# A written plan for the attention steps of the late tiles, on one core

## The chip, the cores and the metric

The kernel runs on one core of a Trainium2 chip. The metric is the time of one execution on the device in microseconds (us), as the median of several runs. Profiles show one execution; PE is TensorE, DVE VectorE, ACT ScalarE, POOL GpSimd, SP SyncE.

## The reference

Pooled attention feeds two feed-forward layers, all in float32:

```python
# q, k, v: 4 batches, 8 heads, 576 positions, 64 per head; pool 8, so 72 pooled keys
k_p = k.reshape(B, H, 72, 8, D).mean(axis=3)
v_p = v.reshape(B, H, 72, 8, D).mean(axis=3)
scores = scale * q @ k_p.T
attn = exp(scores - max(scores)); attn = attn / (sum(attn) + 1e-9)
x = (attn @ v_p), heads side by side            # 2304 tokens x 512
x = (sigmoid(x @ w_gate) * (x @ w_val)) @ w_out # 512 -> 1536 -> 512
h = x @ w_in                                    # 512 -> 2048
out = (h * tanh(softplus(h))) @ w_out2          # 2048 -> 512
```

## The kernel before

The 2304 tokens are 18 attention tiles of 128 tokens, and for the first feed-forward layer five blocks `j` of 512, 384, 384, 512 and 512 tokens (L68). Every large matrix product is made of three products of high and low parts. Block `j` runs 12 units `f` (`NF`), one for each 128 columns of the hidden layer. A unit (L886 to L921) is three parts: the gate product `pg` (12 matmuls, L583 to L587) and its sigmoid on ACT (L893); the value product `pv` (12 matmuls), the gating product on DVE (L899), the high part `gh` on ACT (L902) and the low part `gl` on DVE (L906); and the out product of the unit before (`emit_out`, 12 matmuls, L103 to L105). `pg` and `pv` take two PSUM buffers in turn (`ps_mm`, `bufs=2`).

After each part stand `step(j, f, k)` (L797) and `slot(3f+k)` (L851): 36 parts in a block. `step` first calls `flush` (L553), which runs what is in `later` and moves `soon` to `later`; so a thing put into `soon` in a part's slot is run two parts later, one put into `later` one part later. In blocks 2 and 3 `step` also converts the second layer's weights, one in four parts: `l` loads a raw tile on SP (L209), `c` scales it on ACT (L223), `a` joins its bits on DVE (L232, L237), `b` stores it on SP.

`slot` runs attention for the tiles of block j+1 while block j is computed. In block 0 it follows a plan written by hand (`START`). In blocks 1 to 3 it takes a list of tasks (`att_tasks`, L523, and `batch_tasks`, L360, for the keys and values of a new batch) and spreads it evenly over the 36 parts. A tile's tasks are, in order: scores on PE and row extremes on DVE (L407, L418); exponentials on ACT (L430); normalisation on DVE (L441 to L444); `att_planes`, which clears a tile on DVE (L503) and splits the 32-bit numbers into 16-bit halves on ACT (L506); two empty tasks, in which `att_turn` (L508) issues a transposing DMA on SP; `att_join` on ACT (L521), which joins the halves again; an empty task; and `att_values_out` (L481), the product with the values on PE for one or two tiles and their split into high and low parts. A batch's keys are loaded (L270), summed in groups of 8 on DVE (L276) and scaled (L280); its values are loaded (L346) and summed on DVE (L354) or POOL (L356 to L358). Key loads, value loads and queries have two buffers each.

The raw weights, the planes (`pl`), the transposed planes (`plt`) and the blocks' results (`xs`) share three buffers of one tag, `raw`. All loads and stores of these stages, the first layer's out weights (`wo`, L591) among them, are issued on SP in the order of the program.

In block 1 the old list put the steps into these parts: scores of tile 7 and keys 0, 1 loaded in 1, exponentials in 2, normalisation, keys 0, 1 pooled and keys 2, 3 loaded in 4, split in 5, keys 2, 3 pooled in 6, join in 9, values out in 12. In block 2, for tile 11: scores 8, exponentials 9, normalisation 10, split 11, transpose 13, join 14, values out of tiles 10 and 11 in 16; for tile 13: 26, 27, 28, 29, 31, 32, 34.

## Time and profile before

| what | value |
|---|---|
| median of 3 runs | 898.4 us (895.49 to 900.6) |
| profiled execution | 894.53 us, its span 892.6 us |
| granted clock of PE | 1.00 |
| busy in the span | PE 877.4, DVE 527.7, ACT 457.2, POOL 82.4 us |
| blocks 1, 2, 3 of the first layer | 138 to 222, 222 to 306, 306 to 411 us |

A timeline row gives the start, the duration, the engine, the line, the operation with its output and inputs, the shape and how many instructions are merged in it. What stands in brackets at the end is the idle time of that engine just before it, and whom it waited for. Rows of PE overlap, because matmuls are pipelined: what one costs is the distance from start to start.

### The profile page before, as it was taken

The page shows a single profiled execution, that of the slowest core. Times are in us where ns is not written, and L with a number is a line of the kernel's source. Part 1 is how long each engine was busy: PE and PEld are TensorE (multiplying, and loading weights), DVE is VectorE, ACT ScalarE, POOL GpSimd, SP SyncE. Part 2 cuts the span into 40 slices and gives each one's busy share as a digit, 9 for nine tenths or more (in the row PEclk, how much of TensorE's full clock was granted, in tenths as well). Part 3 has the DMA queues.
Part 4 walks back from the last instruction along what each step waited for, and adds up shares of the span by engine and source line. Part 5 has one row for each costly group of instructions (what it writes and reads, how often), then busy time and mean ns, then how long its engine had stood idle before and what let it go on. Part 6 is the DMA issues. An engine that isn't in the chain of part 4 may idle for free.

```text
span 892.6 us, 12631 instructions
## 1 busy us (share of the span) xinstructions
PE 877.4 (98%) x4692; PEld 781.6 (88%) x4692; DVE 527.7 (59%) x1001; ACT 457.2 (51%) x1035; POOL 82.4 (9%) x90
## 2 busy tenths in 40 slices
PE   8999999999989999999999999999999999999998
PEld 8877889899979988888888899998899998999986
DVE  6889864432644433332668477776677767677632
ACT  7756664355565656454445344455444445444431
POOL 3566430200020000000000000000000000000000
PEclk9999999999999999999999999999999999999999
DMA  7788753744686656345675231212021203110001
GB/s 271 231 301 265 223 189 131 192 134 132 171 264 191 203 167 215 120 119 189 212 242 172 70 122 47 81 48 70 26 83 48 83 24 95 60 48 24 1 35 36
DMA packets 65241, 119.08 MB, mean 133 GB/s; under 512 B 28700, under 2 KB 33564, under 8 KB 65180
## 3 DMA queue, kind: packets, MB, share of 16 engines
q1 hardware_dynamic: 63884, 116.02, 41.4%
q10 hardware_dynamic: 1296, 2.26, 0.7%
q8 instruction: 37, 0.61, 0.3%
q14 instruction: 24, 0.20, 0.1%
HBM read 92.42 MB, written 20.07 MB: 126 GB/s over the span
## 4 chain that ended last, share of the span: by engine, by line
PE 86%; ACT 5%; DMA 4%; DVE 3%; issue 1%; POOL 0%; SPq 0%; ACTq 0%; DVEq 0%
PE acc L966 22%; PE p L105 7%; PE p L103 7%; PE p L104 7%; PE acc L103 5%; PE acc L104 5%; PE acc L105 5%; PE pv L583 4%; PE pg L583 4%; PE pg L584 4%; PE pv L584 4%; PE pv L587 4%; PE pg L587 4%; ACT e L430 2%; PE pv L463 2%; PE sc L407 1%
## 5 line engine op out<-in xcount | busy, mean ns | idle before, releaser
L966 PE MATMUL acc<-w,g 128*128 128x512 f32 x864 | 201.1, 390 | 0.0
L966 PEld LDWEIGHTS acc<-w,g 128*128 128x128 f32 x864 | 161.9, 188 | 32.6
L899 DVE TENSOR_TENSOR sg<-sg,pv 128x512 f32<-128x512 f32 (+1 forms) x58 | 36.5, 629 | 124.4 <-PE pv L587 104.9
L103 PE MATMUL acc<-gh,wo 128*128 128x512 f32 (+1 forms) x240 | 90.0, 375 | 0.0
L104 PE MATMUL acc<-gl,wo 128*128 128x512 f32 (+1 forms) x240 | 88.6, 369 | 0.6 <-DVE gl L744 0.6
L583 PE MATMUL pv<-xh,wv 128*128 128x512 f32 (+1 forms) x232 | 85.8, 370 | 2.7 <-DVE sg L899 2.7
L583 PE MATMUL pg<-xh,wg 128*128 128x512 f32 (+1 forms) x232 | 86.3, 372 | 2.1 <-ACT sg L893 2.1
L105 PE MATMUL acc<-gh,wo 128*128 128x512 f32 (+1 forms) x240 | 88.3, 368 | 0.0
L584 PE MATMUL pg<-xl,wg 128*128 128x512 f32 (+1 forms) x232 | 85.2, 367 | 0.0
L584 PE MATMUL pv<-xl,wv 128*128 128x512 f32 (+1 forms) x232 | 85.1, 367 | 0.0
L902 ACT CAST gh<-sg 128x512 fp32r<-128x512 f32 (+1 forms) x60 | 34.8, 580 | 89.0 <-DVE sg L899 89.0
L103 PE MATMUL p<-top,w2s 128*128 128x384 f32 x216 | 72.5, 336 | 0.0
L105 PE MATMUL p<-top,w2s 128*128 128x384 f32 x216 | 72.4, 335 | 0.0
L104 PE MATMUL p<-top,w2s 128*128 128x384 f32 x216 | 72.3, 335 | 0.0
L893 ACT ACTIVATE sg<-pg 128x512 f32<-128x512 f32 (+1 forms) x58 | 31.9, 550 | 65.4 <-PE pg L587 65.2
L237 DVE SCALAR_TENSOR_TENSOR cv<-raw,cv 128x512 uint32<-128x512 uint32 x68 | 55.9, 822 | 2.3
L587 PE MATMUL pv<-xh,wv 128*128 128x512 f32 (+1 forms) x232 | 56.9, 367 | 0.0
L587 PE MATMUL pg<-xh,wg 128*128 128x512 f32 (+1 forms) x232 | 56.9, 367 | 0.0
L223 ACT ACTIVATE cv<-raw 128x512 f32<-128x512 f32 x66 | 44.8, 679 | 22.9 <-DMA raw<-wo 6.5
L906 DVE TENSOR_TENSOR gl<-sg,gh 128x384 fp32r<-128x384 f32 (+1 forms) x48 | 31.5, 656 | 40.0 <-ACT gh L902 40.0
L583 PEld LDWEIGHTS pv<-xh,wv 128*128 128x128 f32 x232 | 43.6, 188 | 9.4 <-DVE sg L899 3.7
L103 PEld LDWEIGHTS acc<-gh,wo 128*128 128x128 f32 x240 | 45.1, 188 | 6.7 <-issue 1.1
(153 smaller groups left out, 1693.8 us busy)
## 6 DMA issues: line engine op xcount, KB each, us to landing
wo<-wod SPq DMA_DIRECT2D x48, 512.0 KB, 4.9
ws<-w2d SPq DMA_DIRECT2D x24, 512.0 KB, 3.7
raw<-w2i SPq DMA_DIRECT2D x16, 512.0 KB, 3.9
raw<-w2o SPq DMA_DIRECT2D x16, 512.0 KB, 3.5
raw<-wv SPq DMA_DIRECT2D x12, 512.0 KB, 5.6
raw<-wo SPq DMA_DIRECT2D x12, 512.0 KB, 4.4
wod<-wo SPq DMA_DIRECT2D x12, 512.0 KB, 2.6
raw<-wg SPq DMA_DIRECT2D x11, 512.0 KB, 4.2
```

The costliest lines, as they stand in the source:

```text
L103: nc.tensor.matmul(ps, wt[:, 0, cols], xh, start=start, stop=False)
L104: nc.tensor.matmul(ps, wt[:, 0, cols], xl, start=False, stop=False)
L105: nc.tensor.matmul(ps, wt[:, 1, cols], xh, start=False, stop=stop)
L223: eng.activation(out=f32(c), in_=hi, func=AF.Prelu, scale=BIAS, alpha=-(2.0**32))
L237: nc.vector.scalar_tensor_tensor(out=c, in0=lo, scalar=29, in1=c, op0=ALU.logical_shift_right, op1=ALU.bitwise_or)
L583: nc.tensor.matmul(ps[:, c0:c1], w, xh[:, k, c0:c1], start=(k == 0), stop=False)
L584: nc.tensor.matmul(ps[:, c0:c1], w, xl[:, k, c0:c1], start=False, stop=False)
L587: nc.tensor.matmul(ps[:, c0:c1], w, xh[:, k, c0:c1], start=False, stop=(k == KD - 1))
L893: nc.scalar.activation(out=sg, in_=pg[:, :n], func=AF.Sigmoid)
L899: nc.vector.tensor_mul(out=sg, in0=sg, in1=pv[:, :n])
L902: nc.scalar.copy(out=gh, in_=sg)
L966: nc.tensor.matmul(acc[t][0], g[:, a, c], w[:, b, :], start=(f == 0 and first), stop=(f == NF2 - 1 and last),)
```

## The change

The lists of tasks of blocks 1 to 3 are replaced by three written plans of 36 parts, `LATE`. Parts are divided by `|`; a word is a step and its tile (or batch) with a number. `L` loads a key tile, `K` pools it; `U` loads a value tile, `V` sums it (`:p` on POOL, `:v` on DVE); `m`, `M`, `X`, `N` are scores, extremes, exponentials, normalisation; `Q` loads a query tile; `z` clears the planes, now on POOL; `s` splits into them on ACT and puts the transpose into `later`, not `soon`; `j7.0` and `j7.1` are the two halves of a join; `P` is the product with the values. Scores and exponentials of tiles 10 and 14 move to the end of the block before. The first raw load of the second layer's weights moves from part 3 to part 0 of block 2, and each further one from the part of the scaling of the one before (`cl`) to the part in which that one's bits are joined (`al`), so that a load stands three parts ahead of its scaling, not four.

```diff
+LATE = (
+    """
+L2.0 L2.1 m7.0 M7.0 m7.1 M7.1 | X7.0 X7.1 Q9 z7 | N7:v | s7 | K2.0:v | K2.1:v L2.2 L2.3 | U2.0 U2.1
+| j7.0 | j7.1 m8.0 M8.0 m8.1 M8.1 | X8.0 X8.1 Q10 z8 | N8:v K2.2:v | s8 K2.3:v | P7 V2.0:p V2.1:v
+U2.2 U2.3 |  |  | j8.0 V2.2:p V2.3:v U2.4 U2.5 | j8.1 | m9.0 M9.0 m9.1 M9.1 | X9.0 X9.1 Q11 z9 |
+N9:v V2.4:p V2.5:v U2.6 U2.7 | s9 |  | V2.6:p V2.7:v |  |  | j9.0 | j9.1 |  | P8.9 |  |  |  |  |  |
+m10.0 M10.0 m10.1 M10.1 | X10.0 X10.1 Q12
+""",
+    """
+L3.0 L3.1 | N10:v | z10 | s10 | K3.0:v | K3.1:v L3.2 L3.3 | U3.0 U3.1 | j10.0 | j10.1 m11.0 M11.0
+m11.1 M11.1 | X11.0 X11.1 Q13 z11 | N11:v K3.2:v | s11 K3.3:v | V3.0:p V3.1:v U3.2 U3.3 |  | j11.0 |
+j11.1 V3.2:p V3.3:v U3.4 U3.5 | m12.0 M12.0 m12.1 M12.1 | X12.0 X12.1 Q14 z12 | N12:v | s12 | P10.11
+V3.4:p V3.5:v U3.6 U3.7 |  | j12.0 V3.6:p V3.7:v | j12.1 | m13.0 M13.0 m13.1 M13.1 | X13.0 X13.1 Q15
+z13 | N13:v | s13 |  |  | j13.0 | j13.1 |  | P12.13 | m14.0 M14.0 m14.1 M14.1 | X14.0 X14.1 Q16
+""",
+    """
+ | N14:v | z14 | s14 |  |  |  | j14.0 | j14.1 m15.0 M15.0 m15.1 M15.1 | X15.0 X15.1 Q17 z15 | N15:v
+| s15 |  |  | j15.0 | j15.1 | m16.0 M16.0 m16.1 M16.1 | X16.0 X16.1 z16 | N16:v | s16 | P14.15 |  |
+j16.0 | j16.1 | m17.0 M17.0 m17.1 M17.1 | X17.0 X17.1 z17 | N17:v | s17 |  |  | j17.0 | j17.1 |  |
+P16.17 |  |
+""",
+)
...
+            def att_clear(T):
+
+                planes[T] = words("planes")
+                nc.gpsimd.memset(planes[T].bitcast(U32)[:, :, :, SP // 2 :], 0)
+
+            def att_split(T):
+
                 e = e_t[T].bitcast(U16).rearrange("p h (k w) -> p h w k", w=2)
-                h = slice(4 * g, 4 * g + 4)
-                nc.scalar.copy(out=pl_t[T][:, h, :, :SP], in_=e[:, h])
+                for h in (slice(0, 4), slice(4, 8)):
+                    nc.scalar.copy(out=planes[T][:, h, :, :SP], in_=e[:, h])
+                later.append(lambda: att_turn(T))
...
                     i = 3 * f + k + 3 * NF * (j - NBLK + 3)
-                    if i == 3:
-                        w2_step("l")
-                    elif i % 4 == 3 and pos2["c"] < NF2:
-                        w2_step("cl")
+                    if i % 4 == 3 and pos2["c"] < NF2:
+                        w2_step("c")
                     elif i % 4 == 0:
-                        w2_step("a")
+                        w2_step("al" if pos2["l"] <= NF2 else "a")
                     elif i % 4 == 1:
                         w2_step("b")
...
+                if not last:
+                    rows = plan[1:] if j == 0 else [part.split() for part in LATE[j - 1].split("|")]
...
+                    for word in rows[k]:
+                        run(word, j + 1)
```

## Rows read from the trace of the kernel before

**Rows 1.** Busy time by stage: stretch, length, then busy us of PE, PEld, DVE, ACT, POOL.
```profile
138.00:222.00 84.00, 82.03 (x505) 80.39 (x504) 31.85 (x63) 40.84 (x101) 6.31 (x12) 1.00 0.51 144
222.00:306.00 84.00, 79.97 (x487) 77.05 (x485) 38.16 (x80) 51.26 (x128) 7.25 (x12) 1.00 0.69 196
306.00:411.00 105.00, 105.00 (x546) 88.20 (x544) 38.30 (x72) 59.01 (x138) 0.00 (x0) 1.00 0.55 169
```

**Rows 2.** Timeline of PE (start, us, group; idle before in brackets): undisturbed steps.
```profile
152.28 0.85 PE L587 MATMUL pg<-xh,wg 128*128 128x384 f32 x4
152.97 0.33 PE L583 MATMUL pv<-xh,wv 128*128 128x384 f32 x1
...
216.83 1.97 PE L463 MATMUL pv<-pt,vb 72*64 72x128 f32 x32
218.73 0.44 PE L103 MATMUL acc<-gh,wo 128*128 128x384 f32 x1
```

**Rows 3.** Timeline of PE: the five places where it waits in blocks 1 and 2.
```profile
158.52 0.86 PE L587 MATMUL pg<-xh,wg 128*128 128x384 f32 x4
161.35 0.45 PE L583 MATMUL pv<-xh,wv 128*128 128x384 f32 x1 [1.98 <-DVE sg L899]
...
249.34 0.86 PE L587 MATMUL pg<-xh,wg 128*128 128x384 f32 x4
250.92 0.44 PE L583 MATMUL pv<-xh,wv 128*128 128x384 f32 x1 [0.72 <-DVE sg L899]
...
255.04 0.34 PE L105 MATMUL acc<-gh,wo 128*128 128x384 f32 x1
256.57 0.45 PE L583 MATMUL pg<-xh,wg 128*128 128x384 f32 x1 [1.20 <-ACT sg L893]
...
260.96 1.09 PE L463 MATMUL pv<-pt,vb 72*64 72x128 f32 x16
...
264.93 0.44 PE L103 MATMUL acc<-gh,wo 128*128 128x384 f32 x1
...
300.52 0.34 PE L105 MATMUL acc<-gh,wo 128*128 128x384 f32 x1
301.78 0.44 PE L583 MATMUL pg<-xh,wg 128*128 128x384 f32 x1 [0.93 <-ACT sg L893]
```

**Rows 4.** Timeline of DVE at 159 us.
```profile
159.53 0.75 DVE L276 TENSOR_REDUCE kp<-kr 128x72 f32<-128x576 f32 x1 [1.69 <-DMA kr<-kt]
```

**Rows 5.** Timeline of ACT, 244 to 300 us.
```profile
244.43 2.66 ACT L521 COPY pt<-plt 72x512 uint16<-72x512 uint16 x4 [2.21 <-DMA plt<-pl]
246.96 0.48 ACT L893 ACTIVATE sg<-pg 128x384 f32<-128x384 f32 x1
247.45 1.28 ACT L430 ACT_TABLE_LOAD   x1
...
253.47 1.25 ACT L506 COPY pl<-e 128x576 uint16<-128x576 uint16 x2 [1.22 <-DVE e L444]
...
256.03 0.49 ACT L893 ACTIVATE sg<-pg 128x384 f32<-128x384 f32 x1
...
261.88 2.63 ACT L521 COPY pt<-plt 72x512 uint16<-72x512 uint16 x4 [4.23 <-DMA plt<-pl]
...
290.93 0.66 ACT L223 ACTIVATE cv<-raw 128x512 f32<-128x512 f32 x1
...
298.68 1.25 ACT L506 COPY pl<-e 128x576 uint16<-128x576 uint16 x2 [2.86 <-DVE e L444]
```

**Rows 6.** Tile plt, output of the transposing DMA: last line of its answer.
```profile
DMA to landing us min/median/max: 4.3/4.6/7.8
```

**Rows 7.** Timeline of SP: a raw load's issue.
```profile
261.88 0.33 SPq L211 DMA_DIRECT2D raw<-w2i  x1
```

**Rows 8.** Tile raw, the loaded weights: last line of its answer.
```profile
DMA to landing us min/median/max: 3.1/3.9/7.9
```

**Rows 9.** Lines view of POOL: its largest memset (busy, mean ns, idle before).
```profile
L621 POOL MEMSET kb<- 128x576 f32 x2 | 1.1, 577 | 0.0
```

More of the change, by code (lines that the diff above doesn't have):

```diff
@@ L691, in run @@
                     first = a and a[0] < 4
+                    if op in "zsjP":
+                        if op == "z":
+                            att_clear(*a)
+                        elif op == "s":
+                            att_split(*a)
+                        elif op == "j":
+                            att_join(*a)
+                        else:
+                            att_values_out(a, j)
+                        return
                     if op == "L":
@@ L814, in tile_pooled_attention_moe_mish @@
                 last = j == NBLK - 1
-                tasks = []
-                if j == 0:
-                    ready.add(1)
-                elif not last:
-                    o2, n2 = blocks[j + 1]
-                    at = 0
-                    for b in range(o2 // S, (o2 + n2 - 1) // S + 1):
-                        if b not in ready:
-                            ready.add(b)
-                            more = batch_tasks(b)
-                            at = 0 if b * S // 128 == o2 // 128 else len(more)
-                            tasks += more
-                    rows = att_tasks(j + 1)
-                    if at:
-                        both = [y + x for x, y in zip_longest(tasks, rows, fillvalue=[])]
-                        tasks = both
-                    else:
-                        tasks += rows
+                if not last:
+                    rows = plan[1:] if j == 0 else [part.split() for part in LATE[j - 1].split("|")]
                 else:
```

101 lines of the change are left out of this document (23 added, 78 removed).

## The prediction

> **What bounds the kernel now.** I read three views in this order: the busy times by stage, the timeline of PE wherever it shows idle time, and the timelines of ACT, DVE and SP just ahead of those places. The stages first: in unit block 1 (138 to 222 us) PE is busy 82.03 of 84 us, in block 2 (222 to 306 us) 79.97 of 84 us, in block 3 (306 to 411 us) all 105 us [rows 1]. So PE is the bound, the change leaves its instructions as they are, and what can be won is PE's waiting: 1.97 + 4.03 = 6.0 us of visible idle time, all of it in blocks 1 and 2. The second view gives the true size, since a pipelined matmul's row runs on into the gap. Undisturbed, four 384-column matmuls take 0.69 us from start to start, 0.173 us each, and the value product of two tiles takes 218.73 - 216.83 = 1.90 us [rows 2]. Against that cadence the five places lose [rows 3]:
>
> - at 159 us: 161.35 - 158.52 - 0.69 = 2.14 us;
> - at 250 us: 250.92 - 249.34 - 0.69 = 0.89 us;
> - at 255 us: 256.57 - 255.04 - 0.17 = 1.36 us;
> - at 261 us: 264.93 - 260.96 - 1.90 = 2.07 us (the value product);
> - at 301 us: 301.78 - 300.52 - 0.17 = 1.09 us.
>
> That is 7.55 us. I add nothing for the restart of PE after a wait.
>
> **Why PE waits there.** The third view names a cause for each. At 159 us DVE stands 1.69 us on the load of the third or fourth key tile, with the gate product (L899) behind it [rows 4]; the old plan pooled two keys, issued the next two loads and pooled those two parts later. At 250 us ACT stood 2.21 us on the transposing DMA, and the whole join of 2.66 us with the sigmoid behind it came late [rows 5]. At 255 us that delay is still there: sigmoid, exponentials and split stand in one run on ACT, and the run that began at 246.96 delivers the next unit's sigmoid at 256.03 + 0.49 = 256.52, 9.56 us later [rows 5]. At 261 us the join waits 4.23 us for its transpose and the value product two parts behind it has to wait too [rows 5]. At 301 us a weight scaling (0.66 us at 290.93) goes ahead of the exponentials, and the split waits 2.86 us for DVE, which worked on a weight's bits ahead of the normalisation [rows 5].
>
> **The change, part by part.** *Keys.* The new plan loads two keys in part 0, pools them in parts 4 and 5, loads the next two in part 5 and pools them in parts 10 and 11. A part is 12 matmuls of 0.173 us, 2.08 us [rows 2], so even the nearest pair (part 5 to part 10) has 10.4 us. The 2.14 us go.
>
> *Exponentials, normalisation, split.* A unit is three parts, 6.24 us. Gate and value products share two `mm` buffers, so a unit's sigmoid must be done when the next unit's gate product starts, two parts (4.16 us) after its own has ended. For a run on ACT that begins with one unit's sigmoid and ends with the next one's the deadline is 6.24 + 4.16 = 10.4 us after the first gate product's end. The tightest chain of the new plan (X in the first part of a unit, N in the second, s in the third: tiles 8, 9 and 11) is the run that took 9.56 us [rows 5]. So it has 0.84 us to spare if its first sigmoid is on time. The old run at 246.96 began late, behind the join; in the new plan the join of the tile before is over a part earlier. The scaling now falls behind the exponentials, where ACT waits for the normalisation anyway, and DVE's bit work falls behind the normalisation. 1.36 and 1.09 us go, on a margin of 0.84 us. In block 3 a unit is 512 columns wide and the margin grows by a third of 10.4 us.
>
> *Join and value product.* The transpose goes out one part after the split, not two, and the first half of the join follows three to five parts after the split. Transposes landed after 4.3 to 7.8 us, median 4.6 [rows 6]. For tiles 11, 12 and 13 the DMA's issue and the half join stand at least two parts, 4.2 us, apart plus what ACT is behind; the median transpose then arrives about when ACT gets there. The value product comes three to six parts after the first half join, where before it came two parts after the whole, so the 2.07 us go even if a join waits 4 us; the join cut in halves (1.33 us each, of 2.66 [rows 5]) puts a sigmoid between, so 0.89 us go as well.
>
> *Memset on POOL.* Eleven clears leave DVE for POOL, one part or so ahead of their split. POOL is busy 6.31 and 7.25 us of 84 [rows 1] and its largest memset took 0.58 us [rows 9], so they are free as long as POOL is not standing on something else: in front of a clear stand at most some value sums waiting for loads issued three parts earlier. If that cover is gone, the split and the next sigmoid wait: 0 to 0.6 us each, 0 taken.
>
> *Raw weights.* The load now goes out three parts ahead of its scaling, 6.24 us in block 2, against 3.1 to 7.9 us of landing, median 3.9 [rows 8]. It stands on SP directly behind the transpose of the same part, and it needs a buffer of the three that it shares with planes and turned. A load of before began at 261.88 [rows 7], just when ACT was released by the transpose [rows 5]: it had taken the planes' buffer and stood on that DMA, and everything on SP behind it (value loads, `wo` loads) stood too. In the new plan another buffer, that of the raw tile that DVE reads in the same step, comes free about then. Bounds for one round: below, 0; above, transpose plus load, 7.8 + 7.9 - 6.24 = 9.5 us late, of which ACT's slack ahead of the sigmoid (10.4 - 6.24 - 0.5 = 3.7 us) covers part: 5.8 us. I take 0.15 us for each of the four rounds in block 2, near the lower end, because the medians (4.6 + 3.9 - 6.24 = 2.3 us) stay inside the slack: 0.6 us in all.
>
> [...] A load of ACT's table took 1.28 us, and the run of 9.56 us holds two of them [rows 5]. [...]
>
> **The sum.** 7.55 us go and 0.6 us come: 6.95 us less. The profiled execution took 894.53 us (span 892.6 us and 1.9 us around it), so it would take 887.6 us; it was faster than all three timed runs (895.49 to 900.6 us). Taken from their median, 898.4 us, the forecast is 891.4 us.
>
> **Rivals.** *The waits come back in part.* For: a margin of 0.84 us in three places, and transposes or loads near their maxima would use it up. Against: block 3 shows the same work with more room and no wait. Two of the four gains on ACT gone, or 1 us more at each of three tiles: 3 to 4 us of the 7 remain, 894.5 us. *The raw load decides.* If the loads behind the transposes take the planes' buffer, each lands 4.6 + 3.9 = 8.5 us after the transpose's issue, and ACT stands on the scaling with join, gate copy and sigmoid behind it. It decides once a load lands more than 3.7 us late. For: the load at 261.88 [rows 7]; against: the other buffer. At 3 us for each of four rounds in block 2 the 7.55 us turn into 4.5 us lost: 902.9 us. *The waits of the trace are those of one execution.* They come from landing times; if the runs that were timed hold the same work with different waits, the gain may be 2 us: 896.4 us. Against: the causes at 255 and 301 us are order, not landing times. *A switch costs more where ACT is not already behind.* If ACT stood once more for a table load's 1.28 us [rows 5] after each switch, the chain would be 9.56 + 2.56 = 12.1 us, 1.7 us over at tiles 8, 9 and 11: 5.1 us back, 896.5 us. Against: the 9.56 us were measured with ACT working without a pause. [...]
>
> **How the numbers follow.** Forecast 0.64, partly back 0.18, one execution's waits 0.08, switch 0.02, raw load 0.08. The likeliest gives 891.4 us; its own range is 889 to 893.5 us. The range that holds 8 in 10 reaches to the partly-back case and takes in the spread of the timed runs below: 887.5 to 896.5 us. A measurement of this kernel can tell about 0.5%, 4.5 us, from no change; the line is at 893.9 us. Faster by more: 0.68 (the forecast and a little of the next case); within: 0.23; slower by more: 0.09.
>
> **What would show it right or wrong.** Right: PE's busy time in blocks 1 and 2 within 0.5 us of their lengths, and both blocks together some 7 us shorter; ACT's join no longer waiting for the transposing DMA by more than 1 us; no wait of DVE's key pooling. Wrong: PE waiting for a sigmoid in the units of tiles 8, 9 or 11; ACT's scaling of weights waiting for its load in block 2; SP standing on a transpose ahead of a raw load. The prediction also fails if block 0 or the stages after 411 us, which the change does not touch, differ by more than 1 us.

## The result and the profile after

The changed kernel takes 887.39 us in the median of four runs (886.84 to 887.97); the kernel before, run beside it, 897.37 us. The ratio is 0.9885 with an interval of 0.9853 to 0.9917: 1.15% faster. The forecast was 891.4 us with a range from 887.5 us, so the direction held, and so did the bound: what went are PE's waits. Three of the five causes named for them did not hold as named (below), and the time lies 4.0 us under the forecast and 0.1 us under the range.

Busy time by stage of the changed kernel, as in [rows 1]: stretch, length, busy us of PE, PEld, DVE, ACT and POOL, granted clock, DMA share, GB/s.

```profile
138.00:218.00 80.00, 80.00 (x494) 78.61 (x493) 28.24 (x58) 40.40 (x100) 6.88 (x14) 1.00 0.49 144
218.00:299.00 81.00, 81.00 (x532) 79.88 (x532) 38.26 (x80) 54.02 (x133) 8.37 (x16) 1.00 0.73 226
299.00:405.00 106.00, 106.00 (x551) 89.25 (x546) 37.16 (x68) 58.07 (x136) 1.99 (x5) 1.00 0.55 174
```

PE has no idle time left in the three blocks; in [rows 1] 6.0 us were visible. The round stretches of [rows 1] are good for shares, not for lengths. The length of a block is read more exactly from the timeline of PE: from the gate matmul that stands right behind the last out product of the block before (it opens the second unit of a block) to the same matmul of the next block. Here they are for blocks 1, 2, 3 and the last block, before first:

```profile
144.62 0.33 PE L583 MATMUL pg<-xh,wg 128*128 128x384 f32 x1
228.19 0.33 PE L583 MATMUL pg<-xh,wg 128*128 128x384 f32 x1
318.88 0.39 PE L583 MATMUL pg<-xh,wg 128*128 128x512 f32 x1
424.08 0.39 PE L583 MATMUL pg<-xh,wg 128*128 128x512 f32 x1
```

and after:

```profile
146.08 0.33 PE L567 MATMUL pg<-xh,wg 128*128 128x384 f32 x1
227.39 0.33 PE L567 MATMUL pg<-xh,wg 128*128 128x384 f32 x1
312.29 0.39 PE L567 MATMUL pg<-xh,wg 128*128 128x512 f32 x1
417.49 0.39 PE L567 MATMUL pg<-xh,wg 128*128 128x512 f32 x1
```

| stretch | before | after | difference |
|---|---|---|---|
| block 0 (from its first gate matmul, 42.50 and 42.76 us), not changed | 102.12 | 103.32 | +1.20 |
| block 1 | 83.57 | 81.31 | -2.26 |
| block 2 | 90.69 | 84.90 | -5.79 |
| block 3 | 105.20 | 105.20 | 0.00 |
| last block and second layer, to the end of the span | 468.52 | 468.71 | +0.19 |

With the start 0.26 us later that is the whole difference of the two spans, 892.6 - 886.2 = 6.4 us. Blocks 1 to 3 give 8.05 us, where the forecast had 6.95. Block 0 varies by itself: it took between 102.1 and 105.1 us in the profiles of this study, and no kernel changed it.

The chain on ACT that had the smallest margin, at tile 11, is the counterpart of the run in [rows 5] that began at 246.96:

```profile
243.22 0.49 ACT L856 ACTIVATE sg<-pg 128x384 f32<-128x384 f32 x1 [0.93 <-PE pg L571]
...
252.31 0.49 ACT L856 ACTIVATE sg<-pg 128x384 f32<-128x384 f32 x1
...
255.39 1.40 ACT L533 COPY pt<-turned 72x512 uint16<-72x512 uint16 x2 [0.63 <-DMA turned<-planes]
...
257.79 0.67 ACT L245 ACTIVATE cv<-raw 128x512 f32<-128x512 f32 x1 [0.66 <-DMA raw<-w2i]
```

From sigmoid to the end of the next one are 252.31 + 0.49 - 243.22 = 9.58 us, as before (9.56). But the first sigmoid had waited for PE (0.93 us), so it was on time, and 9.58 us end inside the 10.4 us of the deadline. The join waits 0.63 us here for its transpose, against 4.23 us in [rows 5]. Over all tiles, by the answers for the transposed planes and, in block 2, for the raw weights (us, times):

```profile
  DMA turned<-planes: 2.8, 3
```
```profile
  DMA raw<-w2i: 1.8, 3
```

What ACT waits is small, and no PE wait follows from it. The longest wait for a transpose is 1.94 us, at tile 13.

### The profile page after: what moved, and what is told of

Same layout as the page of the kernel before. It is cut to its first block, busy times and chain, and to the rows that moved or that the text cites. A ratio compares the mean times of both kernels' runs of the same rounds, so it can differ in the third digit from the quotient of the medians.

```text
span 886.2 us, 12659 instructions
## 1 busy us (share of the span) xinstructions
PE 875.3 (99%) x4692; PEld 781.7 (88%) x4692; DVE 521.0 (59%) x990; ACT 457.0 (52%) x1035; POOL 86.2 (10%) x101
## 3 DMA queue, kind: packets, MB, share of 16 engines
q10 hardware_dynamic: 1296, 2.26, 0.7%
## 4 chain that ended last, share of the span: by engine, by line
PE 92%; DMA 3%; DVE 2%; ACT 2%; issue 0%; POOL 0%; SPq 0%; ACTq 0%; DVEq 0%
PE acc L929 22%; PE p L127 7%; PE p L125 7%; PE p L126 7%; PE acc L125 5%; PE acc L127 5%; PE acc L126 5%; PE pv L567 5%; PE pg L567 5%; PE pg L568 5%; PE pv L568 5%; PE pg L571 5%; PE pv L571 5%; PE pv L465 2%; PE sc L409 2%; DMA vs<-vt 1%
## 5 line engine op out<-in xcount | busy, mean ns | idle before, releaser
L869 DVE TENSOR_TENSOR gl<-sg,gh 128x384 fp32r<-128x384 f32 (+1 forms) x48 | 30.0, 625 | 38.2 <-ACT gh L865 38.2
L126 PEld LDWEIGHTS acc<-gl,wo 128*128 128x128 f32 x240 | 45.0, 188 | 7.3 <-DVE gl L738 1.7
```

Of the source, the lines that this page charges most:

```text
L126: nc.tensor.matmul(ps, wt[:, 0, cols], xl, start=False, stop=False)
```

## The experiments

Diffs are against the changed kernel unless a line says that they are against the one before. "Block 2" is the length in the profiled execution, read as above. All medians but that of turn_late_again, a single run, come from four or more runs beside runs of the kernel before on the same chip (896.2 to 897.3 us in the median). As that median differs by up to 1.1 us from chip to chip, a difference of 1 us and less between two experiments is read from the lengths of blocks, not from medians.

### The kernel before once more: before_again

No edit.

> The kernel before, unchanged, profiled once more and timed. Theory V (the waits of blocks 1 and 2 differ from execution to execution, and the execution first profiled, 894.53 us, had few of them): times spread over some 5 us (895 to 900 us) against 1.1 us for the changed kernel, and a profile whose time is higher has its excess over 894.5 us in blocks 1 and 2, which then last more than 83.6 + 90.7 us; block 0 and the stages after block 3 within 1 us. Theory B (the excess lies in block 0, where both kernels have waits of 1 to 2 us on DVE): blocks 1 and 2 last 174.3 us again within 1 us and block 0 is 2 to 4 us longer than 102.1 us.

Measured: 895.95 us (ratio 1.0004, 0.9987 to 1.0022); the profiled execution took 897.75 us, 3.2 us more than the first one. Its blocks are 103.14, 83.52, 92.56 and 105.20 us: the five waits stand at the same places, but block 2 is 1.87 us longer. This is theory V for the larger part; 1.02 us lie in block 0 and 0.31 us ahead of it. More on block 2 under the clock, below. What the prediction took for the cause at 250 us falls here and in the first trace alike. On DVE, in the first trace (not among the rows ahead):

```profile
249.72 0.68 DVE L354 TENSOR_REDUCE vb<-vr 72x64 f32<-72x512 f32 x1 [4.55 <-DMA vr<-vt]
250.32 0.54 DVE L899 TENSOR_TENSOR sg<-sg,pv 128x384 f32<-128x384 f32 x1
```

DVE stood 4.55 us on a value load with the gating product behind the sum. PE at 250.92 in [rows 3] waits for exactly that gating product. The sigmoid that the prediction held responsible had ended at 247.44 [rows 5], almost 3 us earlier.

### Value loads and sums

**before_values**, against the kernel before: value loads and sums of a batch are spread over later rows of its list, nothing else.

```diff
-                    [(K, 2), (K, 3), (V, 0), (V, 1)],
+                    [(K, 2), (K, 3)],
+                    [],
+                    [(V, 0), (V, 1)],
+                    [],
+                    [],
+                    [],
+                    [],
...
+                    [],
...
+                    [],
+                    [],
```

> The kernel before with one part of the change alone: a batch's value loads go out later than its keys, and their sums stand in later rows of the list, so that more parts lie between a load and its sum; transposes, joins, splits and raw loads stay as they were. Theory A (DVE standing on value loads with the gating product and the normalisation behind it is the cause at 250 and 255 us): the waits at 250 and 255 us go, 0.9 + 1.4 us and what of the clock hangs on them; 892 to 893.5 us. Rival B (the late join is the cause, as the prediction said): the join still waits for its transpose, the waits stay, 895.5 to 897 us.

Measured: 891.78 us, ratio 0.9948 (0.9931 to 0.9965), 4.4 us less than the kernel before; block 2 takes 86.74 us, 3.95 less. In the order DVE, PE, ACT:

```profile
249.10 0.55 DVE L908 TENSOR_TENSOR sg<-sg,pv 128x384 f32<-128x384 f32 x1 [2.30 <-PE pv L596]
```
```profile
257.65 0.44 PE L592 MATMUL pg<-xh,wg 128*128 128x384 f32 x1 [0.34 <-ACT sg L902]
```
```profile
260.31 2.66 ACT L530 COPY pt<-plt 72x512 uint16<-72x512 uint16 x4 [1.59 <-DMA plt<-pl]
```

The gating product now waits for PE and not PE for it; the wait at 255 us is down to 0.50 us from start to start; the join waits 1.59 us for its transpose, where it waited 4.23, though the transpose is issued by the same rule as before; and the value product at 261 us runs without a gap. So one part of the change carries nearly half of the gain, and three of the five waits came, wholly or mostly, from value loads: theory A. The chain on ACT from sigmoid to sigmoid is still 9.56 us long, but it begins 16.9 us after the start of the block, where it was 18.8. The waits at 159 us (2.06) and 301 us (1.09) stand as they did.

The profiled execution is the slowest of the ten (893.46 us): its block 1 takes 85.07 us, 1.50 more than in the first trace. Behind PE's wait at 161 us the granted clock (the third number from the end) falls:

```profile
164.00:166.00 2.00, 2.00 (x9) 2.00 (x8) 0.13 (x1) 1.83 (x3) 0.00 (x0) 0.55 1.01 332
```

The mean clock of the nine other runs is 0.999 or 1.000, so this is not what the edit does.

**values_tight**: the changed kernel with the value loads and sums of the batch in block 2 as early and as tight as before.

```diff
-L3.0 L3.1 | N10:v | z10 | s10 | K3.0:v | K3.1:v L3.2 L3.3 | U3.0 U3.1 | j10.0 | j10.1 m11.0 M11.0
-m11.1 M11.1 | X11.0 X11.1 Q13 z11 | N11:v K3.2:v | s11 K3.3:v | V3.0:p V3.1:v U3.2 U3.3 |  | j11.0 |
...
+L3.0 L3.1 | N10:v | z10 | s10 | K3.0:v | K3.1:v L3.2 L3.3 U3.0 U3.1 | | j10.0 V3.0:p V3.1:v U3.2 U3.3 | j10.1 m11.0 M11.0
+m11.1 M11.1 | X11.0 X11.1 Q13 z11 V3.2:p V3.3:v U3.4 U3.5 | N11:v K3.2:v | s11 K3.3:v V3.4:p V3.5:v U3.6 U3.7 | | V3.6:p V3.7:v | j11.0 |
...
```

> The changed kernel, but the loads and sums of batch 3's values stand in block 2 where they stood before (parts 5, 7, 9, 11, 13), among the splits and joins. If the old order's late transposes were those that stood on SP behind value loads, the transpose of tile 11 goes out 2 to 4 us later, its join waits, and the time is 1 to 3 us over 887.4 us. Rival (the value loads did no harm): under 0.5 us.

Measured: 893.91 us (0.9959 to 0.9990 of the kernel before), 6.5 us more than the changed kernel; block 2 takes 91.62 us, 6.7 more. DVE, and PE behind it:

```profile
242.69 0.68 DVE L376 TENSOR_REDUCE vb<-vr 72x64 f32<-72x512 f32 x1 [4.22 <-DMA vr<-vt]
...
247.70 0.68 DVE L376 TENSOR_REDUCE vb<-vr 72x64 f32<-72x512 f32 x1 [2.45 <-DMA vr<-vt]
```
```profile
248.90 0.44 PE L567 MATMUL pv<-xh,wv 128*128 128x384 f32 x1 [0.81 <-DVE sg L862]
```

DVE stands on value loads again, and a PE wait for a gating product is back near 250 us. The largest loss, 2.87 us at a sigmoid at 253 us, comes mostly by another path. SP spends 236.01 to 245.43 us on four value loads, a raw load stands behind them, and on ACT the weight scaling ahead of the split waits for it:

```profile
252.73 0.67 ACT L245 ACTIVATE cv<-raw 128x512 f32<-128x512 f32 x1 [3.34 <-DMA raw<-w2i]
```

The kernel before has no such wait there. Behind the 2.87 us the matmuls stand 0.32 us apart, where [rows 2] have 0.173:

```profile
256.77 0.52 PE L568 MATMUL pg<-xl,wg 128*128 128x384 f32 x1
257.09 0.52 PE L567 MATMUL pg<-xh,wg 128*128 128x384 f32 x1
```

The mean granted clock of this execution is 0.998. This is the largest single part that was tried from either side, but not all of it is what the value loads cost in the kernel before.

### When the transpose goes out

**turn_late**: two parts after the split, as before.

```diff
-                later.append(lambda: att_turn(T))
+                soon.append(lambda: att_turn(T))
```

> The changed kernel, but each transposing DMA is issued a part later, as before (joins unmoved). If the earlier transpose is what frees ACT, joins wait 2 to 4 us for the transpose at tiles 11, 12 and 13, and PE waits for sigmoids: 2 to 4 us more, 890 us. Rival (the order of exponentials, normalisation and split, and the distance from join to value product do it): joins wait, but what comes back on PE stays under 1 us, 888 us.

Measured: 891.74 us (0.9931 to 0.9970), 4.35 us more than the changed kernel; block 2 takes 88.36 us, 3.46 more. The answer for the transposed planes (us, times) shows it:

```profile
  DMA turned<-planes: 15.4, 6
```

ACT waits 15.4 us for transposes instead of 2.8. PE loses 0.52 and 0.81 us at sigmoids at 262 and 271 us, and the value product at 299.77 us takes 3.77 us, where the same product took 1.95 us in the kernel before (at 306 us). A part of 2.08 us earlier is worth more than 4 us when joins and products are already placed for it.

**before_turn**, against the kernel before: the transpose one part earlier, nothing else.

```diff
-                        tasks[-1] += [lambda T=T: soon.append(lambda: att_turn(T))]
+                        tasks[-1] += [lambda T=T: later.append(lambda: att_turn(T))]
```

> The kernel before with one thing changed: each transposing DMA is issued a part earlier (later in place of soon). If the late transpose is the cause behind the waits at 250, 255 and 261 us, 3 to 4.3 us of the gain come from this alone: 892.5 to 894 us, and the clock of the runs is higher (0.999 or 1.000). Rival (the order of the steps): under 1 us, 896 us, as many waits as before.

Measured: 899.84 us, ratio 1.0033 (1.0014 to 1.0051): slower. SP, then ACT, at tile 11:

```profile
259.17 0.90 SPq L346 DMA_DIRECT2D vr<-vt  x2
260.17 2.95 SPq L511 DMA_TRANSPOSE plt<-pl  x1
```
```profile
264.91 2.64 ACT L521 COPY pt<-plt 72x512 uint16<-72x512 uint16 x4 [4.93 <-DMA plt<-pl]
```

The transpose stands on SP behind two value loads and goes out at 260.17, 29.99 us after the start of the block; in the kernel before it was 29.06 us (257.25). The join waits 4.93 us, and the value product takes 5.63 us. Earlier in the program is not earlier on the queue.

**before_values_turn**: before_values with the earlier transpose and the later raw loads (the edits of before_turn, and the reverse of load_early below).

> The same with two more parts of the change: the transpose goes out one part after the split and the raw weights are loaded a part later. What is left of the change is the order of exponentials, normalisation and split, the clears and the spacing of the keys. Theory A: with the value loads out of its way on SP the earlier transpose now helps, where alone it made the kernel before slower (899.8 us); 888 to 890.5 us. Rival B: the order on ACT and the late value product are what counts, and the kernel stays within 2 us of the one with the value loads alone, or above it.

Measured: 893.66 us (0.9955 to 0.9992), 1.9 us more than before_values: by the time, rival B. The joins wait 5.2 us in all, hardly less than the 5.6 us of before_values, and PE waits for a sigmoid:

```profile
258.09 0.44 PE L592 MATMUL pg<-xh,wg 128*128 128x384 f32 x1 [1.97 <-ACT sg L900]
```

The transpose of tile 10 goes out 10.94 us after the start of the block here, and 9.86 us in before_values: DVE now clears the planes behind a weight's bit work (clear at 240.33), and the transpose follows at 240.83. So it was not earlier, and what an earlier transpose is worth without the rest of the plan stays open. The parts of this change are not a sum.

### When the raw weights are loaded: load_early

```diff
-                    if i % 4 == 3 and pos2["c"] < NF2:
-                        w2_step("c")
+                    if i == 3:
+                        w2_step("l")
+                    elif i % 4 == 3 and pos2["c"] < NF2:
+                        w2_step("cl")
...
-                        w2_step("al" if pos2["l"] <= NF2 else "a")
+                        w2_step("a")
```

> The changed kernel, but the raw loads of the second layer's weights stand where they stood before (with the scaling, four parts ahead). The forecast put 0.6 us as the price of the later load: undoing it gives 886.8 us. Rival: with the load beside two live tiles of the three buffers it waits for a transpose, SP stands, and scaling or joins on ACT come late: 1 to 4 us more, 888.5 to 891.5 us.

Measured: 889.76 us (0.9909 to 0.9948), 2.4 us more than the changed kernel; block 2 takes 85.65 us. SP, then ACT:

```profile
291.88 1.93 SPq L522 DMA_TRANSPOSE turned<-planes  x1
...
296.16 0.33 SPq L233 DMA_DIRECT2D raw<-w2i  x1
```
```profile
296.16 1.40 ACT L533 COPY pt<-turned 72x512 uint16<-72x512 uint16 x2 [4.11 <-DMA turned<-planes]
```

The early load stands on SP until the transpose has landed and is issued in the same moment in which ACT is released: a load placed four parts ahead is not ahead, and it holds SP. This is the picture of [rows 7]. The later load costs nothing here; it saves. Of the 2.4 us, 0.75 lie in block 2. The profile has another 0.90 us in a wait at 516 us in the second layer, but the profiles of before_turn, before_values_turn and turn_late_fill have 0.8 to 0.9 us at the same place, so that is hardly the load; the rest is open.

### The keys

**keys_tight**: keys pooled and loaded as tight as before.

```diff
-L2.0 L2.1 m7.0 M7.0 m7.1 M7.1 | X7.0 X7.1 Q9 z7 | N7:v | s7 | K2.0:v | K2.1:v L2.2 L2.3 | U2.0 U2.1
+m7.0 M7.0 m7.1 M7.1 | L2.0 L2.1 X7.0 X7.1 Q9 z7 | N7:v | s7 | K2.0:v K2.1:v L2.2 L2.3 |  | K2.2:v K2.3:v U2.0 U2.1
...
```

> The changed kernel, but keys are loaded and pooled as close together as before: two pooled and the next two loaded in part 4, those pooled in part 6 (block 2: parts 3 and 5). If the key loads cost what the forecast took off for them, PE waits 1.5 to 2.5 us for the gating product on DVE in block 1 and the time is 1.5 to 2.5 us over the changed kernel's 887.4, some 889.5 us. Rival: the wait at 159 us needed the split and transpose of the old order beside it (they filled SP and DVE): then no wait over 0.5 us and 887.4 us.

Measured: 887.79 us (0.9886 to 0.9933), 0.4 us more than the changed kernel; block 1 takes 81.92 us, 0.61 more. That is the rival: DVE waits, and yet PE loses only 0.30 us, at a sigmoid at 173 us:

```profile
157.42 0.75 DVE L298 TENSOR_REDUCE kp<-kr 128x72 f32<-128x576 f32 x1 [2.29 <-DMA kr<-kt]
```

**keys_turn**, against keys_tight: the split of tile 7 a part later, so that its transpose goes out behind the key loads.

```diff
-m7.0 M7.0 m7.1 M7.1 | L2.0 L2.1 X7.0 X7.1 Q9 z7 | N7:v | s7 | K2.0:v K2.1:v L2.2 L2.3 |  | K2.2:v K2.3:v U2.0 U2.1
+m7.0 M7.0 m7.1 M7.1 | L2.0 L2.1 X7.0 X7.1 Q9 z7 | N7:v |  | s7 K2.0:v K2.1:v L2.2 L2.3 |  | K2.2:v K2.3:v U2.0 U2.1
```

> The keys as tight as in the run keys_tight, and besides the split of tile 7 a part later, so that its transposing DMA goes out behind the loads of keys 2 and 3 and not ahead of them, as in the kernel before. Theory A (the 2.1 us at 159 us are not the spacing alone: the load of the fourth key lands late beside the transposing DMA): DVE stands twice, the second time over 1 us on the last key, PE waits 1.5 to 2 us for the gating product where keys_tight lost 0.31 us, block 1 takes 83 to 83.8 us against 81.9 us, and the whole 889 to 890 us. Rival B (the transpose has no part in it; the rest of the new plan gives the keys more room): block 1 as in keys_tight, 81.9 us, and 887.5 to 888.5 us.

Measured: 889.34 us (0.9905 to 0.9946), 1.95 us more than the changed kernel; block 1 takes 82.90 us, 1.59 more. DVE, then SP:

```profile
156.38 0.75 DVE L298 TENSOR_REDUCE kp<-kr 128x72 f32<-128x576 f32 x1 [1.19 <-DMA kr<-kt]
...
158.62 0.75 DVE L298 TENSOR_REDUCE kp<-kr 128x72 f32<-128x576 f32 x1 [1.06 <-DMA kr<-kt]
```
```profile
153.57 1.55 SPq L292 DMA_DIRECT2D kr<-kt  x2
...
155.77 4.32 SPq L522 DMA_TRANSPOSE turned<-planes  x1
```

Half right for theory A. DVE does stand twice, and the last key is there 158.62 - 153.57 = 5.05 us after the issue, with the transpose issued behind the loads; this is the picture of [rows 4]. In keys_tight DVE waits once, and the last key is there when the one before it has been pooled. But PE doesn't wait at the gating product; the time goes later, 1.13 us at a sigmoid at 174 us, behind the late join. In the kernel before, normalisation and a clear stood on DVE among the pooling as well, which the new plan also removed:

```profile
152.46 0.76 DVE L444 TENSOR_TENSOR e<-e,sm 128x576 f32<-128x576 f32 x1
...
155.66 0.43 DVE L503 MEMSET pl<- 128x448 uint32 x1
```

DVE waits as long for the keys in all three kernels: 2.24 us before, 2.29 in keys_tight, 2.25 in keys_turn. But from the low part of the unit before (L906, L869) to the gating product behind the keys it takes 9.20 us before, 7.60 and 7.52 us in the other two. The 1.6 us between them are these two steps (1.1 us up to the first pooling, and 0.43), and they are most of what PE lost at 159 us. That share was read from rows and not tried alone.

### Order and margin on ACT

**order_13**: tile 13's scores to split back into the parts of the kernel before; transpose and join as in the new plan. The product of tiles 12 and 13 and the first steps of tile 14 move one part with them.

```diff
-V3.4:p V3.5:v U3.6 U3.7 |  | j12.0 V3.6:p V3.7:v | j12.1 | m13.0 M13.0 m13.1 M13.1 | X13.0 X13.1 Q15
-z13 | N13:v | s13 |  |  | j13.0 | j13.1 |  | P12.13 | m14.0 M14.0 m14.1 M14.1 | X14.0 X14.1 Q16
+V3.4:p V3.5:v U3.6 U3.7 |  | j12.0 V3.6:p V3.7:v | j12.1 |  |  | m13.0 M13.0 m13.1 M13.1 | X13.0 X13.1 Q15
+z13 | N13:v | s13 |  |  | j13.0 | j13.1 | P12.13 | m14.0 M14.0 m14.1 M14.1
...
- | N14:v | z14 | s14 |  |  |  | j14.0 | j14.1 m15.0 M15.0 m15.1 M15.1 | X15.0 X15.1 Q17 z15 | N15:v
+X14.0 X14.1 Q16 | N14:v | z14 | s14 |  |  |  | j14.0 | j14.1 m15.0 M15.0 m15.1 M15.1 | X15.0 X15.1 Q17 z15 | N15:v
```

> The changed kernel with tile 13's scores, exponentials, normalisation and split two parts later, in the parts in which the kernel before has them: a weight scaling stands ahead of the exponentials on ACT and a weight's bit work ahead of the normalisation on DVE. Its transpose and join follow as early as in the changed kernel. Theory A (the 1.1 us at 301 us were the order alone): PE waits 0.9 to 1.3 us for a sigmoid behind the split of tile 13, the rest of block 2 stays, 888.3 to 889.3 us. Rival B (the wait came from being late already, and has no place in the new plan): no wait there, within 0.3 us of the changed kernel, 887.4 to 888 us.

Measured: 888.55 us (0.9894 to 0.9949), 1.16 us more; block 2 takes 86.06 us, 1.16 more. ACT, then PE:

```profile
293.78 1.25 ACT L516 COPY planes<-e 128x576 uint16<-128x576 uint16 x2 [2.88 <-DVE e L446]
```
```profile
296.88 0.45 PE L567 MATMUL pg<-xh,wg 128*128 128x384 f32 x1 [0.95 <-ACT sg L856]
```

These are the rows of [rows 5] at 298.68 and [rows 3] at 301.78, to 0.02 us. The cause at 301 us is order alone.

**split_heavy**: the split's copies are made three times for tiles 8, 9 and 11.

```diff
-                for h in (slice(0, 4), slice(4, 8)):
-                    nc.scalar.copy(out=planes[T][:, h, :, :SP], in_=e[:, h])
+                for _ in range(3 if T in (8, 9, 11) else 1):
+                    for h in (slice(0, 4), slice(4, 8)):
+                        nc.scalar.copy(out=planes[T][:, h, :, :SP], in_=e[:, h])
```

> The changed kernel, but the split of tiles 8, 9 and 11 is done three times over on ACT (four copies more, 2.5 us). The forecast gave the chain from sigmoid to sigmoid 9.56 of 10.4 us, 0.84 us to spare: PE then waits 1.7 us for a sigmoid at each of the three tiles, 5 us in all, 892.4 us. Rival (there is more room than the sum says, 2 us or over): under 1.5 us in all, 888.5 us.

Measured: 892.04 us (0.9924 to 0.9961), 4.65 us more. ACT, then PE, at tile 9:

```profile
189.78 3.54 ACT L517 COPY planes<-e 128x576 uint16<-128x576 uint16 x6 [1.78 <-issue]
```
```profile
195.17 0.45 PE L568 MATMUL pg<-xh,wg 128*128 128x384 f32 x1 [1.61 <-ACT sg L857]
```

A split of 3.54 us, 2.29 more than 1.25, makes PE lose 1.78 us here, 1.79 at tile 11 and 0.54 at tile 8, so between 0.5 and 1.75 us were free: the margin of 0.84 us was of the right size. The changed kernel's chain of 9.58 us holds two loads of ACT's table:

```profile
243.73 1.28 ACT L432 ACT_TABLE_LOAD   x1
245.03 0.32 ACT L432 ACTIVATE e<-sc,mx 128x72 f32<-128x72 f32 x1
...
249.75 1.25 ACT L516 COPY planes<-e 128x576 uint16<-128x576 uint16 x2 [1.23 <-DVE e L446]
251.01 1.28 ACT L856 ACT_TABLE_LOAD   x1
252.31 0.49 ACT L856 ACTIVATE sg<-pg 128x384 f32<-128x384 f32 x1
```

Each takes 1.28 us, and 0.02 us after it the next activation starts. ACT did pause in this chain, 1.23 us for DVE (1.22 us in [rows 5]), so the 9.56 us of the prediction were not measured without a pause. PE has no wait at tiles 8, 9 and 11 without the edit.

### The value product: value_early

```diff
-j11.1 V3.2:p V3.3:v U3.4 U3.5 | m12.0 M12.0 m12.1 M12.1 | X12.0 X12.1 Q14 z12 | N12:v | s12 | P10.11
+j11.1 V3.2:p V3.3:v U3.4 U3.5 | P10.11 m12.0 M12.0 m12.1 M12.1 | X12.0 X12.1 Q14 z12 | N12:v | s12 |
```

> The changed kernel, but the value product of tiles 10 and 11 stands in part 16 of block 2, one part after the second half of tile 11's join, as near as before. Theory of the forecast (the wait at 261 us came from the short distance from join to value product): PE waits there, 1.5 to 2.5 us, time 889 to 890 us. Rival (it came from the late transpose, which the new plan sends earlier): under 0.7 us there, 887.4 to 888 us. If short waits inside the value product also lower the granted clock, the runs' mean clock falls under 0.999.

Measured: 893.39 us (0.9934 to 0.9966), 6.0 us more; block 2 takes 89.56 us. At the product itself PE loses 0.39 us, as the rival has it (under 0.7 us there). What cost more was new:

```profile
263.45 2.29 PE L409 MATMUL sc<-kb,q 128*128 128x144 f32 x8 [2.68 <-DVE xl L497]
```

The scores of tile 12, now right behind the product, had to wait until DVE had emptied the product's PSUM. In all ten runs the mean granted clock was under 1.000 (0.996 to 0.998). The price in time of an early product alone stays open. In order_13 the product of tiles 12 and 13 stands one part behind the second half of its join too, and PE shows no wait there: with the earlier transpose the short distance costs 0 to 0.4 us.

### The clears: clear_dve

```diff
-                nc.gpsimd.memset(planes[T].bitcast(U32)[:, :, :, SP // 2 :], 0)
+                nc.vector.memset(planes[T].bitcast(U32)[:, :, :, SP // 2 :], 0)
```

> The changed kernel with the clears of the planes on DVE, where they were before, in the parts of the new plan. On POOL they wait for buffers (for stores and loads to land) with nothing behind them; on DVE the gating product stands behind them. If that matters, PE waits for the gating product or the sigmoid, 1 to 5 us more; rival (0.43 us each on an engine with room): 887.4 us within 0.5 us.

Measured: 888.05 us (0.9866 to 0.9929). That is the rival, by the lengths of the blocks: 1, 2 and 3 of the profile are 81.31, 84.90 and 105.20 us, the same as in the changed kernel to 0.01 us; the median is 0.66 us higher. The engine of the clear is worth nothing where it now stands.

### The clock

**turn_late_again** and **turn_late_more** are turn_late once more, for a second profile and for more runs. 

> A second profile of the changed kernel with the transposes a part later. In three of its four timed runs the mean clock was 0.997, in the profiled one 1.000, at the same time (891.4 to 892.0 us). If a clock that falls costs the time it takes at half speed, a run at 0.997 has 2.7 us of it and must have less waiting elsewhere; the profile shows where. Rival: the clock falls where PE has little to do, and costs nothing.

> turn_late once more, for the comparison with turn_late_fill on one chip: 891.5 to 894.5 us, mean clock 0.996 to 0.998 in most runs.

The two profiles of the same program, turn_late and turn_late_again, differ by 2.14 us in block 2 (88.36 and 90.50), with similar waits at the product (it takes 3.77 and 4.12 us), and one wait of 0.52 us less in the second. Stages of the second:

```profile
302.00:306.00 4.00, 3.71 (x24) 3.45 (x25) 1.78 (x3) 1.88 (x4) 0.00 (x0) 0.54 0.75 256
306.00:310.00 4.00, 4.00 (x18) 4.00 (x18) 1.79 (x5) 1.76 (x3) 0.00 (x0) 0.60 0.04 15
```

From the stretched value product on the granted clock is 0.54 and 0.60; in the first profile it stayed 1.00. turn_late_more gave 892.1 us, and its runs order themselves: 889.5 to 890.4 us in the three with a mean clock of 0.999 or 1.000, 892.1 to 893.7 us in the four from 0.995 to 0.998. The four runs of turn_late do not: 891.97 us at 1.000 and 891.4 to 891.95 us at 0.997. The fall is seen in before_again too, PE and then its stages:

```profile
264.24 0.44 PE L463 MATMUL pv<-pt,vb 72*64 72x128 f32 x4 [0.39 <-ACT pt L521]
...
268.45 0.52 PE L105 MATMUL acc<-gh,wo 128*128 128x384 f32 x1
268.77 0.52 PE L103 MATMUL acc<-gh,wo 128*128 128x384 f32 x1
```
```profile
262.00:266.00 4.00, 3.17 (x33) 1.95 (x31) 0.31 (x1) 2.57 (x5) 0.70 (x2) 1.00 1.03 303
...
268.00:270.00 2.00, 2.00 (x8) 2.00 (x7) 1.97 (x5) 0.51 (x2) 0.00 (x0) 0.50 0.18 74
...
272.00:274.00 2.00, 2.00 (x13) 2.00 (x13) 0.00 (x0) 0.49 (x1) 0.00 (x0) 1.00 0.92 309
```

Behind the product that waits for joins, matmuls stand 0.32 us apart where [rows 2] have 0.173, at a granted clock of 0.50 (268 to 270 us); from 272 to 274 us it is 1.00 again. That is most of the 1.87 us by which this block 2 is longer.

The 105 runs of the kernel before that belong to the experiments (before_again and those beside the others), with a median of 896.56 us:

| mean granted clock | runs | median us |
|---|---|---|
| 1.000 | 18 | 894.77 |
| 0.999 | 12 | 895.37 |
| 0.998 | 29 | 896.58 |
| 0.997 | 16 | 896.62 |
| 0.996 | 20 | 897.97 |
| 0.995 and less | 10 | 898.1 to 900.1 by step |

A straight line through them falls 0.78 us for each 0.001, with a correlation of -0.75; 0.001 of 895 us would be 0.9 us. In before_again both came in one execution, a longer wait (1.66 us for 0.89 at 250 us) and matmuls at 0.50, so this is not the price of the clock alone.

**turn_late_fill** puts matmuls into PE's waiting time, against turn_late:

```diff
+                        for _ in range({4: 5, 6: 2}.get(h, 0) if T == 13 and t0 == 0 else 0):
+                            nc.tensor.matmul(ps[:, 128:256], ident, ident, start=True, stop=True)
```

> The changed kernel with late transposes (turn_late), plus seven matmuls of the identity into the part of tile 13's PSUM buffer that its last heads overwrite: five ahead of its heads 4 to 7, where PE waited 1.02 us for the join, two ahead of heads 6 and 7, where it waited 0.29 us. They fill waiting time and make nothing shorter. If the clock that falls behind these waits is a matter of PE standing idle, the runs' clock stays at 0.999 to 1.000 where turn_late's lay at 0.996 to 0.997, and the time is 1 to 3 us below that of turn_late_more on the same chip. Rival (the clock falls for another reason): as low a clock, and a time up to 0.5 us higher.

Measured: 892.44 us, beside 892.1 us of turn_late_more on the same chip. The mean clock is 0.999 or 1.000 in all six runs, so the fall is gone; the time is not lower.

**before_fill** does it in the kernel before, in the products at 261 and 306 us.

```diff
+                        for _ in range({0: 4, 2: 2, 4: 2, 6: 2}.get(h, 0) if idle is not None and t0 == 0 else 0):
+                            nc.tensor.matmul(idle, ident, ident, start=True, stop=True)
...
-                    att_pv(T, g, ps=ps[:, 256 * g : 256 * g + 256])
+                    att_pv(T, g, ps=ps[:, 256 * g : 256 * g + 256], idle=ps[:, 384:512] if T in (11, 13) else None)
```

> The kernel before with 10 small matmuls of the identity matrix added within the value products of tiles 10 with 11 and 12 with 13, where PE stands waiting for joined tiles; what they write is overwritten and no order is changed. Theory A (about 3 of the 10 us are a lower granted clock after these stuttering products): the mean granted clock is 0.999 to 1.000 in most runs and the median 894.5 to 895.5 us, 1 to 2.5 us less than the kernel before. Rival B (the clock has little to do with it, or these waits do not bring its fall): the same spread of clocks and a median within 0.5 us of the kernel before, or above it by the price of the added matmuls, some 0.1 us each where they delay.

Measured: 900.35 us, ratio 1.0039 (1.0022 to 1.0057). The clock came out as theory A has it, 0.998 to 1.000 in all twelve runs and 1.000 in seven; the time went the other way. The profile tells why:

```profile
263.32 0.44 PE L465 MATMUL pv<-pt,vb 72*64 72x128 f32 x4
263.69 0.71 PE L463 MATMUL pv<-ident 128*128 128x128 f32 x4
264.33 0.44 PE L465 MATMUL pv<-pt,vb 72*64 72x128 f32 x4
```

A step of the product with its fill takes 264.33 - 263.32 = 1.01 us, more than the join takes for the next two heads (0.62 us from step to step in the first trace). The product grew from 3.97 to 5.52 us, and the one at 306 us, which had not waited, to 5.56 us from 1.95: 5.2 us, nearly all that block 2 grew (95.96 against 90.69).

So in these two kernels the fall of the clock is all but gone when PE is kept busy inside those products (0.999 or 1.000 in six runs, 0.998 to 1.000 in twelve). What it costs is known only from executions that differ in it, and no fill earned it back.

## Why the prediction was right and where it failed

**The bound and what could be won.** Right. PE has no wait left in blocks 1 to 3. The sum said 7.55 us of waits would go; 8.05 us went in those blocks. The forecast for the profiled execution was 887.6 us, and after's profiled execution took 887.97 us. So near a hit is in part luck: the blocks gave 1.10 us more than the 6.95 us, and block 0, which the change leaves alone, took 1.20 us more in this execution.

**The step that failed** stands in the sum: "Taken from their median, 898.4 us, the forecast is 891.4 us". The 6.95 us were read from an execution with a granted clock of 1.00 and were taken off a median that lies 3.9 us higher, as though that excess belonged to work that the change leaves alone. It did not. Some 1.8 us of it are the small sample: the median of 105 runs is 896.56 us, where that of three was 898.4. Another 1.8 us go with the granted clock: the runs of the kernel before that have a mean clock of 1.000 take 894.77 us. That is 7.4 us more than the changed kernel, in which four of four runs have 0.999 or 1.000, so the sum itself, 6.95 us, was 0.4 us short. The low clock comes behind waits that the change removes (0.50 in before_again, 0.55 in before_values), so its share of the excess goes with them. How much of these 1.8 us is the clock itself and how much is longer waits in the same runs stays open: in before_again slow matmuls make most of the 1.87 us of block 2, but its wait at 250 us is longer too (1.66 for 0.89 us), and no run changes the clock alone. The range failed with it: its lower end was set at the very time that the profile's own sum gave.

**Terms of the sum that were mis-sized or had another cause.**

- *Keys, 2.14 us.* The time went (block 1 is 2.26 us shorter), but the spacing that was given the credit is worth 0.4 us in the time and 0.61 us in the block. DVE waits as long for the keys when they are tight again, and PE does not wait for the gating product. What the sum left out is DVE's own work among the pooling, 1.6 us of normalisation and clear, by the rows. The transpose behind the key loads costs another 1.0 us in block 1, at a sigmoid behind the late join and not at the gating product.
- *250 us, 0.89 us.* The cause named was the join on ACT. It was DVE on a value load with the gating product behind it; before_values removes the wait and leaves the join whole.
- *255 us, 1.36 us.* "That delay is still there" was right as a chain: it is 9.56 us long in before_values too. But what made it begin late were mostly the same value loads: 0.50 us are left in before_values, where it begins 1.9 us earlier in the block.
- *261 us, 2.07 us.* The product did wait for the join and the join for its transpose. The remedy named was an earlier transpose; before_turn shows that alone it loses, since it stands behind value loads on SP and goes out later. Without these the old transpose is early enough for this product.
- *301 us, 1.09 us.* Right, shown by order_13 at 1.16 us.
- *Raw loads, +0.6 us.* Wrong in sign. Both bounds were costs; the gain, an end of SP's standing on the transposes, was seen in [rows 7] and not given a number. load_early shows 0.75 us of it in block 2; the medians differ by 2.4 us, and the rest is open.
- *Clears, 0.* Right: clear_dve.
- *Restart after a wait, 0.* Small: order_13 loses 1.16 us where PE is idle 0.95.

The value loads, the largest part, have no term of their own in the prediction. They appear in it only where they stand in front of something on SP or POOL. The list of what each engine does just before PE's wait ought to have been read on DVE at 250 us as it was at 159 us.

**The rivals.** Partly back and the raw load did not happen: no wait for a sigmoid at tiles 8, 9 or 11, and the raw loads were waited for 1.8 us in all. (In values_tight a raw load did decide, by 2.87 us, because it stood behind value loads.) The dearer table switch did not happen either: the chain with two table loads took 9.58 us, not 12.1. "The waits of the trace are those of one execution" was right in its premise and wrong in its direction: other executions had more to lose than the profiled one, not less.

**The signs named ahead.** PE's busy time and the key pooling came as the right sign has them. Others did not: one join waited 1.94 us for its transpose, over the 1 us that was named, and ACT's scaling waited for its load in block 2 three times, a sign of being wrong. SP, too, still spends 1.8 to 2.0 us on each transpose of block 2 with a raw load right behind it. PE lost nothing by any of them. "The prediction also fails if block 0 or the stages after 411 us ... differ by more than 1 us": block 0 is 1.20 us longer in after's profile. By its own words the test is failed. Block 0 was 103.14 us in before_again too, so this is its own scatter, and the bound of 1 us was too narrow for it.

## What to carry to other kernels

When a profiled execution is faster than the timed runs, ask what those have more of before taking a saving off their median: here a granted clock of 0.50 stood behind waits of the bounding engine (before_again), and in the changed kernel, without these waits, all four runs have a mean of 0.999 or 1.000. A median of three runs can lie 1.8 us off that of a hundred. For each wait, read the row just before it on every engine in the chain, and on the queue that issues the loads; in before_turn two value loads that stand on SP in front of a transpose left the join on ACT waiting 4.93 us and the value product on PE at 5.63 us. Parts of a written plan don't add up: the transpose placed a part earlier lost 3 us alone, where it went out no earlier, and was worth 4 us in company.

## What the runs showed of the hardware

A granted clock of about half came in before_again behind a group of waits of PE (1.66, 1.13 and a product that stretched from 1.90 to 3.72 us, within 16 us; 0.50 from 268 to 270 us), in turn_late_again from a product on that took 4.12 us (0.54 from 302 to 306 us), and in before_values behind a single wait, 2.06 us at 161 us (0.55 from 164 to 166 us). In values_tight, behind 0.98 and 2.87 us, matmuls stand 0.32 us apart as they do at 0.50 in before_again. It did not come in the first profile of the kernel before, behind 2.14 us at the same place and the same group (1.00 in every 2 us from 160 to 168 and from 254 to 270 us), nor in split_heavy, which has waits of 0.54, 1.78 and 1.79 us and a mean clock of 1.000 in nine of ten runs and 0.999 in the profiled one. The same program can show the fall in one execution and not in the next (turn_late 1.00, turn_late_again 0.54). What decides is not shown.

The issue of a transposing DMA held SP for 1.7 to 5.2 us in the kernel before, where that of a raw load as in [rows 7] takes 0.33 to 0.85 us (ns, min/median/max, from the answers for the transposed planes and the raw weights):

```profile
L511 SPq DMA_TRANSPOSE plt<-pl x11: 1705/1917/5201, 156.9 to 402.0; - x11
```
```profile
L211 SPq DMA_DIRECT2D raw<-w2i x16: 332/378/848, 230.6 to 386.3; - x16
```

What stands behind it on SP waits for that time: the `wo` load behind the longest one was issued 5.31 us after that one's start.

```profile
156.88 5.20 SPq L511 DMA_TRANSPOSE plt<-pl  x1
162.19 0.52 SPq L591 DMA_DIRECT2D wo<-wod  x1
```
